# Sums for the next pair of chunks at earlier steps, a fixed order of products in every group, and a later flag matmul

## The chip, the cores and the metric

The kernel runs on one core of a Trainium2 chip. The metric is the device time of one execution in microseconds (us); for the kernel before it is 1270.25 us, the median of 3 runs (1269.96 to 1272.42). TensorE (PE) multiplies, VectorE (DVE), ScalarE (ACT) and GpSimd (POOL) do the elementwise work, and SyncE (SP) issues almost all DMAs. Each engine has one queue of instructions that it works off in order, and semaphores hold an instruction until what it needs is done.

## The reference

Three layers follow each other, all in float32:

```python
state = alpha[t] * state + k[t] v[t]^T ; y[t] = q[t] @ state        # linear attention, 4 x 8 heads, 768 x 48
x = y as [3072, 384]
h = x @ w_in ; g = where(h > 0, h, exp(min(h, 0)) - 1) ; x = g @ w_out        # w_in [384, 2048]
p = domain_probs / (domain_probs.sum(-1) + 1e-9)
for e in range(4):
    out += p[:, e:e+1] * (maximum(x @ w1[e], 0) @ w2[e])        # w1 [4, 384, 1024], w2 [4, 1024, 384]
```

## The kernel before, in words

The sequence is cut into 6 chunks of 128 positions times 4 batches, so 512 tokens are one chunk. Stage 1 (0 to about 530 us) runs attention and the first feed-forward layer. Stage 2, to which the change belongs, runs the four experts. It takes the chunks in three pairs, r = 0, 1, 2. The hidden units of all experts are cut into 32 blocks of 128, and 11 groups q = 0 to 10 take three blocks each (the last takes two). So there are 33 groups, numbered i = 11 r + q; group 12, for instance, is r = 1, q = 1.

The first product of a group (`layer1`, its matmuls are on line L810) is not done block by block, but by a scheme with fewer multiplications: 15 steps (`STEPS`; 11 steps, `STEPS2`, for q = 10), each of which multiplies one combination of weights by one combination of x and adds the product b to running tiles S0 to S5 (called `u`) or writes one of six results `c`. Results are named (m, f): half m of the tokens, block f. They come in the order (1,2) at step 5, (1,0) at step 8, (1,1) at step 10, (0,2) at step 12, (0,1) at step 13, (0,0) at step 14. All operations that read b run on VectorE, and so does S5 - at step 7 `S5 = S4 - S2`, which reads no b. Only `S1 = S1 - S4` at step 7 and `c(1,0) = S3 + S0` at step 8 run on GpSimd. At step 13 VectorE does `S1 = S1 + b`, so it needs GpSimd's S1.

The products are kept exact by splitting: every product is a main one (L810 or L870 with f32 operands, from the `xh` or `gh` tiles) and two corrections (f16 operands, from `xc` or `gc`). For a result c, ScalarE writes the main part `gh` (L755), the rectified c in place (L756) and one half of `gc` (L758), and GpSimd writes the other half of `gc` (L760).

The second product of group i - 1 (`layer2`, L870) runs interleaved with the steps of group i, as 18 items (12 for q = 10), each one main product and two corrections; the first step has no item, the second as a rule two, which read (1,0) and (1,1). `extra(n, 0)` issues items ahead of step n's matmuls and `extra(n, 1)` behind them. The switch `self.wide` decides which: when it is 0, mains go ahead, then the step's main and corrections, then the items' corrections; when it is 1, corrections go first and mains last. It flips with every step, so products of one kind lie next to each other. It is set to 0 once, at i = 0. As all groups have 15 or 11 steps, even groups begin with 0 and odd groups with 1, and the last pass (i = 33, only `layer2`) with 1.

When the last block of an expert is done, `gate` multiplies each of six banks by the probabilities on VectorE (L887) and adds it to `acc` on GpSimd (L890); for the last expert the sum is stored (L892, `out_dram`). For r = 0 that happens in groups 11 and 12.

The 15 combinations of x for the next pair are made by `prep_x(r + 1)`. It is a list of 16 pieces: piece 0 loads the raw chunk pair (`load`, L595, four DMAs into `xraw`), pieces 1 to 15 each make one combination (`one`): GpSimd adds 0 to 3 terms (L674, `xv`), two flushes later ScalarE casts it (L679, L680, `xh`), one flush after that GpSimd subtracts (L683) and SP stores it (L684, `xcd`). Groups q = 1 to 8 put in two pieces each, at steps 2 and 9. In q = 1 these are the load and combination 14, which has three additions. Only r = 0 (group 1) and r = 1 (group 12) prepare a next pair.

The order of PE, ACT, DVE and POOL is the order in which the program emits the work. SP's order is chosen by the planner of the framework, which may bring a DMA forward; once chosen, SP works it off in order too. Weights are loaded per group, `wa` (L727) and `wb` (L737) from step 0.

At the end, `flag` reduces range checks with small VectorE operations (L907 to L919), `total` sums them over the partitions by a tiny matmul (L923) into the value `ok`, which all engines read (L1306) before the program ends.

Of the kernel before, what the change touches and what calls it, by code (L numbers as in the profile page):

```python
# [95 lines left out]
class _Fast:  # L96
# [833 lines left out]
    def run(self):  # L930
# [129 lines left out]
        def second(it, ks=range(KD)):  # L1060
            g = gs[it]
            c, f = it
            self.g2a(self.w1[f // 2], f % 2, g, 512, f == 0, f == F1 - 1, ks)
            if KD - 1 in ks:
                del gs[it]
                if f == F1 - 1:
                    self.later(lambda: end1(c))
# [40 lines left out]
        for i in range(ng + 1):  # L1108
            r, q = divmod(i, NG)
            work, first_work = [], {}  # L1110
            if i:
                self.hb = ("h0", "h1")
            if i == 0:
                pieces = [(it, k) for it in items[-LA:] for k in range(KD)]
                first_work = dict(zip((4, 7, 9, 11, 13, 14), pieces))
            elif i > 0:
                work = self.layer2(i - 1, G.pop(i - 1))
            if i == ng:
                while self.queue:
                    self.flush()  # L1120
                total = self.flag()
                for n in range(0, len(work), 2):
                    if n == 4:
                        total()
                    for k in range(2):
                        for f in work[n:n + 2]:
                            f(k ^ self.wide)
                    self.flush()
                    self.wide ^= 1
                break  # L1130
            if i == 0:
                self.wide = 0
                self.hacc = self.wp.tile([128, 256], F32, tag="wt", name="hacc")
                self.hc, self.wc = 0, [0, 0]
            steps = len(STEPS if q < NG - 1 else STEPS2)
            plan = {}
            put = lambda n, f, *a: plan.setdefault(n, []).append((f, a))
            if i <= NG:
                for n, f in enumerate(self.bound_w(i)):
                    put(2 * n + 1, f)  # L1140
            if i >= 2:
                put(0, self.load_wb, i)
            if 1 <= i < ng - 1:
                put(0, self.load_wa, i + 1)
            if q in (1, 3, 6, 8):
                put(steps - 1, self.load_pb, r, (1, 3, 6, 8).index(q))
            if r + 1 < NPR:
                if q == 1:
                    xs = self.prep_x(r + 1)
                if 1 <= q <= 8:  # L1150
                    for n, s in enumerate(xs[(q - 1) * 2:q * 2]):
                        put(2 + 7 * n, do, s)
                if q == NG - 2:
                    put(4, self.load_xc, r + 1, 0)
                if q == NG - 1:
                    for j in range(1, 5):
                        put((2, 5, 8, 9)[j - 1], self.load_xc, r + 1, j)

            dve = [sum(1 for o in ops if "b" in o[2:] or o[1] == "S5") for _, ops in (STEPS if q < NG - 1 else STEPS2)]
            cum = [0]  # L1160
            for n in range(steps):
                cum.append(cum[-1] + 1 + dve[n] + (dve[n - 1] if n else 0))
            cut = [len(work) * c // cum[-1] for c in cum]

            def extra(n, k):
                for f in work[cut[n]:cut[n + 1]]:
                    f(k ^ self.wide)
                if k == 0:
                    return
                self.wide ^= 1  # L1170
                if n in first_work:
                    second(first_work[n][0], (first_work[n][1],))
                for f, a in plan.pop(n, []):
                    f(*a)

            G[i] = self.layer1(i, extra)
            assert not plan
# [186 lines left out]
```

## Time and profile before

| what | value |
|---|---|
| median of 3 runs | 1270.25 us |
| the profiled execution's own time | 1268.04 us |
| its span, first to last instruction | 1266.3 us |
| PE busy | 1226.3 us (97%), 6453 instructions |
| DVE busy | 901.2 us (71%) |
| ACT busy | 785.7 us (62%) |
| POOL busy | 555.3 us (44%) |
| mean granted TensorE clock | 0.993 of full speed |

The profile is of one execution on the chip. "Busy" is the time in which an engine worked on an instruction. PE's matmuls are pipelined, so a share of 97% says that it was rarely idle, not that it ran at its peak. The granted clock is 1.0 when TensorE has its full 2.4 GHz and 0.5 at 1.2 GHz. In rows of the timeline, the first column is the start in us from the span's start, the second the time from the first instruction's start to the last one's end, then engine, line, operation, tiles (out<-in) with shapes, and the count of instructions merged; brackets give the idle time of the engine before it and who ended it.

### The profile page before, as it was taken

What the parts mean: (1) busy time and instruction counts of PE and PEld (TensorE: products, weight loads), DVE (VectorE), ACT (ScalarE), POOL (GpSimd) and SP (SyncE); (2) the same over time, 40 slices, a digit from 0 to 9 for tenths busy, and PEclk for the clock granted to TensorE, in tenths of its full rate; (3) what the DMA queues carried; (4) which work ended last, traced back from release to release, by engine and by line L of the source; (5) the groups of instructions that cost most, each with busy time, mean ns of one, the idle gap of its engine ahead of it and who ended that gap; (6) DMA issues with size and microseconds to landing.
All of it is one profiled execution on the core that took longest, in us unless ns stands there. A gap on an engine that the chain in (4) does not pass through costs nothing. (4 is left out here: it accounts for less than half of the span.)

```text
span 1266.3 us, 18550 instructions
## 1 busy us (share of the span) xinstructions
PE 1226.3 (97%) x6453; PEld 801.3 (63%) x6457; DVE 901.2 (71%) x1478; ACT 785.7 (62%) x1624; POOL 555.3 (44%) x496
## 2 busy tenths in 40 slices
PE   8899999999999999999999999999999999999995
PEld 5677878888787888755555555555555555555553
DVE  8999687786787868866666657676766566667763
ACT  5675666766656667678787766466565455464552
POOL 0000011110111114267777957776878474456654
PEclk9899999999999999999999999999999999999998
DMA  6655356555656456735564677855555875343321
GB/s 234 234 169 170 99 194 198 191 188 188 227 199 219 159 185 218 277 125 217 180 222 162 219 253 286 291 198 219 196 203 204 301 256 191 117 177 140 143 94 53
DMA packets 78101, 246.84 MB, mean 195 GB/s; under 512 B 6840, under 2 KB 38424, under 8 KB 69936
## 3 DMA queue, kind: packets, MB, share of 16 engines
q1 hardware_dynamic: 77136, 240.87, 54.2%
q10 hardware_dynamic: 864, 4.72, 0.9%
q8 instruction: 52, 0.85, 0.3%
q14 instruction: 49, 0.40, 0.1%
HBM read 182.21 MB, written 63.36 MB: 194 GB/s over the span
## 5 line engine op out<-in xcount | busy, mean ns | idle before, releaser
L833 DVE TENSOR_TENSOR u<-h,u 128x512 f32<-128x512 f32 x258 | 177.4, 688 | 83.1 <-PE h L810 79.8
L760 POOL TENSOR_TENSOR gc_W<-c,gh_W 128x512 f16<-128x512 f32 x128 | 164.6, 1287 | 162.1 <-ACT c L756 117.6
L396 POOL TENSOR_SCALAR wh<-wc 128x384 f16<-128x384 f32 (+1 forms) x55 | 31.2, 567 | 406.6 <-ACT wh L395 349.5
L870 PEld LDWEIGHTS <-wb 128*128 128x128 f16 x1152 | 112.4, 98 | 141.3 <-issue 7.2
L755 ACT ACTIVATE gh_W<-c 128x512 fp32r<-128x512 f32 x128 | 80.3, 627 | 159.3 <-POOL c L833 85.8
L810 PE MATMUL h<-xc_Q,wa 128*128 128x512 f16 x520 | 155.6, 382 | 1.1 <-DVE c L833 0.7
L810 PE MATMUL h<-xh_Q,wa 128*128 128x512 f32 x260 | 127.0, 489 | 1.5 <-DVE u L833 1.3
L756 ACT ACTIVATE c<-c 128x512 f32<-128x512 f32 x192 | 121.1, 631 | 7.6 <-ACT gh_W L755 0.4
L810 PEld LDWEIGHTS <-wa 128*128 128x128 f16 x780 | 60.5, 98 | 100.9 <-issue 55.4
L833 DVE TENSOR_TENSOR c<-u,h 128x512 f32<-128x512 f32 x123 | 84.3, 686 | 51.2 <-PE h L810 35.2
L760 POOL TENSOR_TENSOR gc_X<-c,gh_X 128x512 f16<-128x512 f32 x64 | 82.7, 1292 | 70.9 <-ACT c L756 68.2
L462 DVE SCALAR_TENSOR_TENSOR h<-e,h 128x512 f32<-128x512 f32 x96 | 66.4, 692 | 63.9 <-ACT e L461 63.6
L827 DVE COPY u<-h 128x512 f32<-128x512 f32 x99 | 67.9, 690 | 51.5 <-PE h L810 48.4
L870 PE MATMUL t<-gc_W,wb 128*128 128x512 f16 x384 | 97.3, 379 | 0.9 <-POOL gc_W L760 0.9
L755 ACT ACTIVATE gh_X<-c 128x512 fp32r<-128x512 f32 x64 | 40.2, 627 | 80.7 <-POOL c L833 44.9
L467 ACT CAST g<-h 128x512 fp32r<-128x512 f32 x96 | 56.0, 583 | 51.1 <-DVE h L462 50.8
L468 DVE TENSOR_TENSOR g<-h,g 128x512 fp32r<-128x512 f32 x96 | 65.7, 684 | 26.0 <-ACT g L467 25.8
L460 ACT ACTIVATE e<-h 128x512 f32<-128x512 f32 x96 | 57.0, 593 | 41.1 <-PE h L451 41.0
L758 ACT CAST gc_W<-c 128x512 f16<-128x512 f32 x128 | 79.2, 619 | 4.0
L476 PE MATMUL t<-g,w_W 128*128 128x512 f32 x324 | 79.4, 389 | 0.0
L810 PE MATMUL h<-xc_W,wa 128*128 128x512 f16 x260 | 77.8, 382 | 1.1 <-DVE u L833 1.0
L890 POOL TENSOR_TENSOR acc<-acc,c 128x512 f32<-128x512 f32 x53 | 69.4, 1321 | 2.7 <-DVE c L887 2.7
(264 smaller groups left out, 2935.7 us busy)
## 6 DMA issues: line engine op xcount, KB each, us to landing
wa<-wad SPq DMA_DIRECT2D x33, 1536.0 KB, 6.7
wb<-wbd SPq DMA_DIRECT2D x30, 1536.0 KB, 7.1
raw<-in_att_dram SPq DMA_DIRECT2D x22, 964.0 KB, 5.7
wad<-wh SPq DMA_DIRECT2D x44, 384.0 KB, 2.8
wbd<-wh SPq DMA_DIRECT2D x43, 384.0 KB, 4.0
xcd<-xh SPq DMA_DIRECT2D x30, 512.0 KB, 2.9
wraw<-in_wm_dram SPq DMA_DIRECT2D x16, 768.0 KB, 5.0
wraw<-in_we_dram SPq DMA_DIRECT2D x20, 576.0 KB, 5.1
```

The costliest lines, as they stand in the source:

```text
L462: return lambda: nc.vector.scalar_tensor_tensor(out=h, in0=e, scalar=-1.0, in1=h, op0=ALU.add, op1=ALU.max)
L468: return g, lambda: nc.vector.tensor_tensor(out=g[:, 1], in0=h, in1=g[:, 0].bitcast(F32), op=ALU.subtract)
L476: nc.tensor.matmul(self.xa[k][:, 0:n], w[wl][:, fi, DM + k * 128:DM + (k + 1) * 128], g[:, gl, 0:n], start=(first and i == 0), stop=(last ...
L755: nc.scalar.activation(out=hi, in_=v, func=AF.Relu, scale=s)
L756: nc.scalar.activation(out=v, in_=v, func=AF.Relu, scale=s, accum_out=self.hacc[:, self.hc:self.hc + 1])
L758: nc.scalar.copy(cor[:, 0], v)
L760: lambda: nc.gpsimd.tensor_tensor(out=cor[:, 1], in0=v, in1=hi.bitcast(F32), op=ALU.subtract)
L810: nc.tensor.matmul(b, u, v, start=(j == 0), stop=(j == 2))
L827: nc.vector.tensor_copy(out, b)
L833: (nc.vector if "b" in (a0, a1) or dst == "S5" else nc.gpsimd).tensor_tensor(out=out, in0=val(a0, b), in1=val(a1, b), op=ALU.add if op == ...
L870: nc.tensor.matmul(oa[m, d], w, g, start=n == 0 and k == 0, stop=n == F2 - 1 and k == 2)
L890: eng.tensor_tensor(out=acc, in0=acc, in1=t, op=ALU.add)
```

## The change

Three edits, all in stage 2. (1) The pieces of `prep_x` move from steps 2 and 9 of a group to steps 1 and 4. (2) `self.wide` is set to 0 at the start of every group and of the last pass, so every group begins with main products. (3) In the last pass, `total` is emitted ahead of the last two of the 12 items instead of ahead of items 4 and 5.

```diff
@@ the last pass, i == ng @@
                 total = self.flag()
+                self.wide = 0
                 for n in range(0, len(work), 2):
-                    if n == 4:
+                    if n == 10:
                         total()
@@ the start of a group @@
             if i == 0:
-                self.wide = 0
                 self.hacc = self.wp.tile([128, 256], F32, tag="wt", name="hacc")
                 self.hc, self.wc = 0, [0, 0]
+            self.wide = 0
@@ the plan of a group @@
                 if 1 <= q <= 8:
                     for n, s in enumerate(xs[(q - 1) * 2:q * 2]):
-                        put(2 + 7 * n, do, s)
+                        put(1 + 3 * n, do, s)
```

## Rows read from the trace of the kernel before

**Rows 1.** Windows: stage 2; busy of PE, PEld, DVE, ACT, POOL, then granted clock
```profile
531.00:1226.00 695.00, 685.76 (x3068) 374.95 (x3068) 458.76 (x692) 429.32 (x921) 470.41 (x362) 1.00 0.56 200
```

**Rows 2.** Waits of PE from 545 us on: total, times, longest
```profile
PE h L810 <- DVE u L833: 3.5, 4, 1.4
PE a L870 <- POOL gc_W L760: 2.8, 3, 1.6
PE h L923 <- DVE flag_r L919: 2.2, 1, 2.2
...
PE t L870 <- POOL gc_W L760: 0.9, 1, 0.9
...
PE h L810 <- DVE u L827: 0.7, 2, 0.3
```

**Rows 3.** Timeline of SP: around group 1's raw loads, and in group 12
```profile
525.56 1.69 SPq L595 DMA_DIRECT2D xraw<-x1d  x2
...
789.67 4.08 SPq L892 DMA_DIRECT2D out_dram<-acc  x2
793.86 0.41 SPq L737 DMA_DIRECT2D wb<-wbd  x1
794.32 5.73 SPq L595 DMA_DIRECT2D xraw<-x1d  x4
```

**Rows 4.** Timeline of POOL in group 12
```profile
792.08 1.27 POOL L890 TENSOR_TENSOR acc<-acc,c 128x512 f32<-128x512 f32 x1
796.56 1.30 POOL L760 TENSOR_TENSOR gc_W<-c,gh_W 128x512 f16<-128x512 f32 x1 [3.20 <-ACT c L756]
797.81 1.77 POOL L833 TENSOR_TENSOR u<-u 128x512 f32<-128x512 f32 x1
...
804.79 1.28 POOL L674 TENSOR_TENSOR xv<-xraw 128x512 f32<-128x512 f32 x1 [1.17 <-DMA xraw<-x1d]
806.91 2.64 POOL L674 TENSOR_TENSOR xv<-xv,xraw 128x512 f32<-128x512 f32 x2 [0.84 <-DMA xraw<-x1d]
```

**Rows 5.** Timeline of DVE and of ACT at the end of group 12
```profile
806.38 0.68 DVE L833 TENSOR_TENSOR u<-h,u 128x512 f32<-128x512 f32 x1
...
800.86 0.63 ACT L755 ACTIVATE gh_W<-c 128x512 fp32r<-128x512 f32 x1 [3.73 <-POOL c L833]
...
802.80 0.62 ACT L755 ACTIVATE gh_W<-c 128x512 fp32r<-128x512 f32 x1
```

**Rows 6.** Timeline of PE at the start of groups 12 and 13
```profile
785.37 0.50 PE L810 MATMUL h<-xh_W,wa 128*128 128x512 f32 x1 [1.36 <-DVE u L833]
...
807.74 0.59 PE L810 MATMUL h<-xc_W,wa 128*128 128x512 f16 x2
...
810.84 1.02 PE L870 MATMUL a<-gc_W,wb 128*128 128x512 f16 x4 [0.70 <-POOL gc_W L760]
```

**Rows 7.** Timeline of PE and windows: two runs of nine matmuls in stage 1
```profile
81.42 2.34 PE L451 MATMUL h<-x,w_W 128*128 128x512 f32 x9
...
88.27 3.83 PE L451 MATMUL h<-x,w_W 128*128 128x512 f32 x9 [2.47 <-DVE g L468]
...
88.00:92.00 4.00, 3.73 (x10) 2.90 (x11) 3.01 (x5) 3.94 (x9) 0.00 (x0) 0.59 0.23 94
```

**Rows 8.** Timeline of POOL and PE at the end of group 1
```profile
565.76 2.63 POOL L674 TENSOR_TENSOR xv<-xv,xraw 128x512 f32<-128x512 f32 x2
...
569.66 0.59 PE L870 MATMUL a<-gc_W,wb 128*128 128x512 f16 x2 [1.56 <-POOL gc_W L760]
```

**Rows 9.** Timeline of DVE and PE in group 30
```profile
1192.74 1.68 DVE L833 TENSOR_TENSOR u<-u 128x512 f32<-128x512 f32 x1
...
1195.68 0.50 PE L810 MATMUL h<-xh_Q,wa 128*128 128x512 f32 x1 [0.56 <-DVE u L833]
```

**Rows 10.** Timeline of PE and of POOL at the end
```profile
1250.75 0.19 PE L923 MATMUL h<-flag_r 128*1 128x4 f32 x2 [2.15 <-DVE flag_r L919]
...
1251.41 6.20 POOL L890 TENSOR_TENSOR acc<-acc,c 128x512 f32<-128x512 f32 x5 [1.76 <-DVE c L887]
```

## The prediction

> **What bounds the kernel now.** I read the shares of the engines first, then the windows, then PE's waits, and last the queues of POOL and SP around the places that the edits touch. From 531 to 1226 us PE is busy for 685.76 of 695.00 us at a granted clock of 1.00, its upper level of 2.4 GHz [rows 1]: stage 2 is bound by TensorE, and a reordering can win only what PE still waits. That is little. From 545 us on the waits sum to about 12 us; POOL's `gc` accounts for 2.8 + 0.9 us, the flag for 2.2 us in one piece, and VectorE's `u` for 3.5 and 0.7 us [rows 2]. So the edits can win some 5 us at most, while one new hole on PE's path costs its full length.
>
> **Edit 1, sums at steps 1 and 4.** What it removes: at the end of group 1 the last two of three additions run for 2.63 us, `gc` comes behind them and PE waits 1.56 us [rows 8]. At step 4 these additions lie before the results begin, and the wait goes. The 0.9 us on `t<-gc_W` (group 6, after a sum at step 9) and the two waits of 0.3 us on L827 behind a full POOL should go too. I take 1.6 + 0.9 + 0.6 = 3.1 us; the bounds are 0 and 4.4 (all of POOL's 2.8 + 0.9 and L827's 0.7) [rows 2].
>
> What it moves is not only the additions. In groups 1 and 12 the first piece is the load of the raw pair and the second needs it: seven steps lay between them, now three. Stage 2's group of 15 steps takes 807.74 - 785.37 = 22.4 us [rows 6], 1.49 us a step, so the distance shrinks from 10.4 to 4.5 us. In group 1 this is harmless: its loads were issued by 527 us, long before [rows 3]. In group 12 they were not. SP issues the four loads at 794.32 to 800.05, directly behind two stores (789.67 to 793.75), which wait for GpSimd's last `acc` (792.08, done 793.35), and a `wb` load [rows 3, 4]. These stores and `wb` are emitted at step 0, before the load whether it stands at step 2 or at step 1, so I expect the loads where they were. The data came at 804.8 and 806.9, where POOL waited 1.17 and 0.84 us for it [rows 4], already late for step 9.
>
> After the change POOL reaches the additions when `acc` is done, at 793.35, waits until 804.8, and is through at 806.91 + 2.64 = 809.55. Queued behind, at 1.3 us each [rows 4]: `gc(1,2)` until 810.8 (before, it ran at 796.56), the `xh` difference until 812.1, S1 until 813.4 (before, from 797.81), `c(1,0)` until 814.7. VectorE needs S1 at step 13, which it did at 806.38 [rows 5]; now it does so at 813.4, done 814.1. PE needs the bank that this frees for the first step of group 13: 814.1 instead of 807.74 [rows 6], 6.4 us. ScalarE is behind `c(1,0)` too: its results follow at 802.80 - 800.86 = 1.94 us [rows 5], so c(1,0) is rectified at 816.0 and (1,1) at 817.9, and GpSimd's `gc(1,1)` is done at 819.2. Group 13 with mains first has its first corrections right behind the first step, so PE waits for that as well, then has two corrections (0.45), the step's three products (0.67) and two mains (0.45) to do, at 685.76 / 3068 = 0.224 us a matmul [rows 1]: 820.8. Before, this point was reached at 810.84 + 0.45 = 811.3 [rows 6]. The price is 9.5 us, group 13's own wait of 0.70 included. Bounds: -0.7 (the data are early, as in group 1) and 9.5; I take 9.5, since the loads' row in group 12 is the nearest.
>
> **TensorE's clock after that hole.** In stage 1, nine matmuls took 2.34 us, and nine like them 3.83 us after PE had waited 2.47 us; the granted clock of that stretch was 0.59, so for most of it the lower level, 1.2 GHz [rows 7]. A hole of 6.4 us, followed by two shorter ones, should do the same: 3.83 - 2.34 = 1.5 us more; bounds 0 (waits of up to 1.6 us in stage 2 left the clock at 1.00 [rows 1, 2]) and 3.0 (twice). The Trainium skill (TensorE: Matmul & The Clock Gate, Why this matters for your kernels) advises against gaps between bursts of matmuls because the clock falls, which speaks against this edit; by it alone the 1.5 us would be owed for the 6.4 us hole and not for the short ones. The rows agree on both.
>
> The moved pieces' other instructions: ScalarE's casts and SP's stores come five steps earlier, where ScalarE idles (3.73 us before a result [rows 5]); at nothing, as PE waits for no weight load that stands behind such a store [rows 2]. But the `xh` difference now lies at step 7, beside VectorE's S5, which reads two SBUF tiles. Group 30 shows such a meeting: S5 took 1.68 us, where such an operation takes 0.68 [rows 5], while POOL ran, a gate followed, and PE waited 0.56 us at step 10 [rows 9].
>
> **Edit 2, mains first.** Odd groups now run like even ones. In these, products of steps 7 and 8 come close together, which is where PE waited for `u` in gate groups (0.56 in group 30). Corrections of the second step are also needed 1.1 us earlier (0.67 + 0.45). I count three more waits of 0.6 us, for gate groups that become even-like or get the `xh` difference beside S5: 1.8 us. Bounds: -0.5 (odd groups' own waits go) and 4.8 (all eight such gate groups: 3, 11, 17, 19, 25 and 8, 14, 6). The order changes kind once more per border, 32 times; kinds change at every step already without a visible wait, so 0.2 us, bounds 0 and 1.
>
> **Edit 3, the flag.** PE no longer stands 2.15 us for the flag's sum [rows 10]. But GpSimd's five additions run back to back from 1251.41 to 1257.61, and they begin when the first gate is done, behind the flag's operations on VectorE, which stay. So the stores become bound by POOL, about half a microsecond before VectorE's last addition now ends (1257.23 + 0.93). With the mains ahead of `gc` I take 0.8 us; bounds -2.2 and +0.3 (`ok` is written some 2 us later, still before the last store).
>
> **Sum.** 9.5 + 1.5 - 3.1 + 1.8 + 0.2 - 0.8 = +9.1 us. The profiled execution took 1268.04 us (span 1266.3 and 1.7 around it), so 1277.1 by its measure. It lies 2.2 us under the median of the runs shown; on that median the sum gives 1279.4 us, which is my forecast.
>
> **Rivals.** (A) *The loads are early.* If SP takes the four loads ahead of the two stores, nothing of the hole is left. The place is SP's queue in group 12. The point: POOL must be through with `gc(1,1)` by 809.5 or so (it follows the additions by 9.7 us), so with the additions by 799.8, 9.75 us earlier than 809.55; so the loads have to begin by about 784.6 instead of 794.32. For it: SP brought group 1's loads forward by more than a group. Against: it did not do so in group 12, with the same freedom. Time: -0.7 - 3.1 + 1.8 + 0.2 - 0.8 = -2.6, 1267.7 us, faster. (B) *The loads come between the two stores*, behind the first (790.1), as the second waits for `acc`: 4 us earlier, so 9.5 becomes 5.5, and the sum 5.1: 1275.4 us. (C) *The small terms cancel*: the loads early, few of POOL's waits gone and more of S5's meetings: 1270 us. (D) *S5's meetings dominate* on top of the hole: 4.8 for 1.8, 1282.4 us.
>
> **How the numbers follow.** Forecast 0.56 (own range 1275.5 to 1282), D 0.05, B 0.12, A 0.19, C 0.08. The range of 1269 to 1283 leaves out most of A and little above, about 2 in 10. A measurement of this kernel can tell about 0.2%, 2.5 us, from no change: slower takes the forecast, D and B without its low end, 0.72; faster takes 0.12 of A, whose 2.6 us lies at the bound; the same takes the rest of A, C and B's low end, 0.16.
>
> **What would show it.** Right: in group 12 POOL stands some 11 us for `xraw` ahead of its first `xv`; PE stands 6 us at the start of group 13 and again at its first corrections, and the granted clock falls there; the wait at 569.66 is gone; L923 no longer waits 2 us. Wrong: SP issues group 12's loads before 785, or POOL's S1 is done before 806; or waits of 0.6 us at step 10 show in many groups.

## The result and the profile after

The changed kernel takes 1287.34 us (median of 4 runs, 1285.58 to 1288.78), the kernel before 1270.11 us beside it (4 runs). The ratio is 1.0135, interval 1.0112 to 1.0157. It became slower, as forecast, but by nearly twice the forecast +9.1 us, and above the range. A second set of 4 runs (e8 below) gave 1283.24 us and a ratio of 1.0115 (1.0081 to 1.0149). Two executions below, 4145 us in e7 (the one that was profiled) and 1771 us in e9, were in a slow state: the medians hold them, the ratios do not.

The profiled execution took 1288.01 us, 19.97 more than the one before. Cutting both traces at the first product of a group (three L810 matmuls a step) shows where:

| part | before | after | difference | forecast |
|---|---|---|---|---|
| stage 1 (start of group 0) | 529.03 | 533.88 | +4.85 | none |
| groups 12 and 13 | 45.21 | 55.27 | +10.06 | +11.0 (hole 9.5, clock 1.5) |
| groups 6 to 9 | 89.98 | 94.44 | +4.46 | |
| groups 16 to 20 | 111.48 | 113.68 | +2.20 | |
| group 2 | 23.73 | 22.41 | -1.32 | |
| groups 0 to 31 less these | 426.34 | 425.73 | -0.61 | |
| the four rows above together | | | +4.73 | -1.1 |
| from the start of group 32 to the end of the span | 40.53 | 40.79 | +0.26 | -0.8 |
| around the span | 1.74 | 1.81 | +0.07 | |

First the view that bounds, stage 2 (busy of PE, PEld, DVE, ACT, POOL, granted clock, DMA share, GB/s), answering to [rows 1]: PE is idle for 18.4 of 715 us (before 9.2 of 695), and the clock is 0.99.

```profile
531.00:1246.00 715.00, 696.57 (x3090) 378.14 (x3089) 462.71 (x695) 432.49 (x929) 469.39 (x363) 0.99 0.55 197
```

PE's waits from 550 us on (total, times, longest), answering to [rows 2]:

```profile
PE h L810 <- DVE u L833: 10.0, 9, 4.3
PE a L870 <- POOL gc_W L760: 4.3, 5, 1.6
PE t L870 <- POOL gc_W L760: 1.7, 3, 1.2
PE a L870 <- POOL gc_X L760: 1.1, 2, 0.8
PE h L810 <- DVE c L833: 0.7, 1, 0.7
PE h L810 <- DVE u L827: 0.5, 1, 0.5
```

One wait of 4.3 us is new, which is the hole. The flag's line has gone. But GpSimd's `gc`, of which I forecast that 2.5 us would go, now costs 7.1 us in 10 waits, against 4.8 in 6: to the 3.7 in 4 of [rows 2] come two lines of before on `gc_X`:

```profile
PE a L870 <- POOL gc_X L760: 0.8, 1, 0.8
...
PE t L870 <- POOL gc_X L760: 0.3, 1, 0.3
```

The hole, in SP's queue in group 12 (answers to [rows 3]):

```profile
795.68 6.58 SPq L892 DMA_DIRECT2D out_dram<-acc  x3
802.37 0.41 SPq L737 DMA_DIRECT2D wb<-wbd  x1
802.82 3.70 SPq L595 DMA_DIRECT2D xraw<-x1d  x4
```

Group 12 begins at 793.87 us here and at 785.37 before [rows 6]. The loads begin 8.95 us into it in both: they stayed behind the stores, as forecast. GpSimd in the same group (answers to [rows 4]):

```profile
800.59 1.27 POOL L890 TENSOR_TENSOR acc<-acc,c 128x512 f32<-128x512 f32 x1
811.48 1.28 POOL L674 TENSOR_TENSOR xv<-xraw 128x512 f32<-128x512 f32 x1 [9.61 <-DMA xraw<-x1d]
813.61 2.64 POOL L674 TENSOR_TENSOR xv<-xv,xraw 128x512 f32<-128x512 f32 x2 [0.86 <-DMA xraw<-x1d]
...
817.43 1.26 POOL L683 TENSOR_TENSOR xh<-xv,xh 128x512 f16<-128x512 f32 x1
818.65 1.26 POOL L833 TENSOR_TENSOR u<-u 128x512 f32<-128x512 f32 x1
```

It stands 9.61 us for the raw data, and S1 (`u<-u`) is behind it. PE at the start of group 13 (answers to [rows 6]), and the windows after its long wait (columns as in the stage 2 row above):

```profile
820.69 0.80 PE L810 MATMUL h<-xh_W,wa 128*128 128x512 f32 x1 [4.28 <-DVE u L833]
...
823.96 1.01 PE L870 MATMUL a<-gc_W,wb 128*128 128x512 f16 x2 [1.59 <-POOL gc_W L760]
825.89 1.01 PE L870 MATMUL a<-gc_W,wb 128*128 128x512 f16 x2 [0.92 <-POOL gc_W L760]
```

```profile
821.00:826.00 5.00, 2.49 (x6) 0.69 (x6) 1.15 (x2) 4.67 (x10) 2.68 (x3) 0.50 0.86 314
826.00:831.00 5.00, 5.00 (x14) 2.48 (x13) 1.53 (x3) 4.79 (x11) 3.19 (x3) 0.55 0.00 0
```

PE stops three times, and its clock is at the lower level to about 830.5 us.

The tail (answers to [rows 10]): L923, the flag's matmul, no longer waits in its row, but GpSimd's five additions begin where they did, 25.66 us after the start of group 32 (before 25.64), and take 6.62 instead of 6.20 us.

```profile
1272.12 0.19 PE L923 MATMUL h<-flag_r 128*1 128x4 f32 x2
...
1271.07 6.62 POOL L890 TENSOR_TENSOR acc<-acc,c 128x512 f32<-128x512 f32 x5 [1.76 <-DVE c L887]
```

### The profile page after: what moved, and what is told of

It is laid out like the page before. It is cut to its first block, busy times and chain, and to the rows that moved or that the text cites. A ratio compares the mean times of both kernels' runs of the same rounds, so it can differ in the third digit from the quotient of the medians.

```text
span 1286.2 us, 18582 instructions
## 1 busy us (share of the span) xinstructions
PE 1236.4 (96%) x6453; PEld 805.1 (63%) x6457; DVE 902.7 (70%) x1478; ACT 785.5 (61%) x1624; POOL 554.2 (43%) x496
## 4 chain that ended last, share of the span: by engine, by line
PE 62%; POOL 13%; DVE 9%; ACT 8%; issue 5%; DMA 2%; SPq 0%; POOLq 0%; DVEq 0%; ACTq 0%
PE h L810 15%; PE t L476 12%; PE h L451 12%; PE t L870 8%; PE a L870 7%; PE h L870 3%; POOL acc L890 3%; POOL gc_W L760 3%; ACT c L756 2%; POOL xh L683 2%; POOL c L833 2%; ACT gh_W L755 1%; POOL xv L674 1%; PE a L259 1%; POOL u L833 1%
## 5 line engine op out<-in xcount | busy, mean ns | idle before, releaser
L810 PE MATMUL h<-xc_Q,wa 128*128 128x512 f16 x520 | 155.6, 382 | 0.0
L810 PE MATMUL h<-xh_Q,wa 128*128 128x512 f32 x260 | 129.1, 497 | 3.8 <-DVE u L833 2.4
L810 PEld LDWEIGHTS <-wa 128*128 128x128 f16 x780 | 60.7, 98 | 97.3 <-issue 50.9
L827 DVE COPY u<-h 128x512 f32<-128x512 f32 x99 | 68.0, 690 | 71.4 <-PE h L810 69.7
L810 PE MATMUL h<-xc_W,wa 128*128 128x512 f16 x260 | 79.2, 387 | 0.0
L810 PE MATMUL h<-xh_W,wa 128*128 128x512 f32 x130 | 68.0, 523 | 7.8 <-DVE u L833 7.8
```

The lines of the kernel that those rows point to most:

```text
L810: nc.tensor.matmul(b, u, v, start=(j == 0), stop=(j == 2))
L827: nc.vector.tensor_copy(out, b)
```

## The experiments

My theory after the result: the late loads make the hole, and the 4.73 us elsewhere come from both edits together (sums that delay GpSimd's S1, and corrections that odd groups need earlier). The rivals were that one of the two edits makes them alone. "Stage 2" below is the time from the start of group 0 to that of group 32 in each kernel's profiled execution, 696.74 us for the kernel before and 711.53 for the changed one (711.31 in e8, the same kernel, so 0.2 us is the scatter that was seen).

| kernel | median us (before beside it) | ratio, interval | stage 2 | groups 6-9 | 12+13 | 16-20 |
|---|---|---|---|---|---|---|
| e1, only edit 1 | 1285.85 (1270.44) | 1.0120, 1.0097 to 1.0142 | 711.99 | 93.81 | 55.80 | 113.63 |
| e2, only edit 2 | 1271.64 (1270.44) | 1.0012, 0.9998 to 1.0026 | 697.23 | 90.99 | 44.43 | 112.35 |
| e3, only edit 3 | 1270.59 (1270.44) | 1.0007, 0.9993 to 1.0022 | 696.77 | 90.04 | 45.22 | 111.49 |
| e4, after + early loads | 1274.56 (1270.44) | 1.0026, 1.0009 to 1.0043 | 700.56 | 94.38 | 44.53 | 113.67 |
| e5, e4 with steps 1, 2 | 1270.82 (1269.77) | 1.0005, 0.9990 to 1.0020 | 697.95 | 92.82 | 44.19 | 113.29 |
| e6, e4 with steps 1, 9 | 1271.62 (1269.77) | 1.0023, 1.0003 to 1.0042 | 697.57 | 91.78 | 44.17 | 112.43 |
| e7, e4 + late differences | 1268.82 (1269.77) | 0.9984, 0.9969 to 0.9999 | - | - | - | - |
| e8, after again | 1283.24 (1269.77) | 1.0115, 1.0081 to 1.0149 | 711.31 | 94.41 | 55.22 | 113.63 |
| e9, e7 again | 1269.35 (1269.95) | 0.9978, 0.9964 to 0.9993 | 693.49 | 90.07 | 44.19 | 111.55 |
| e10, e9 without edits 2, 3 | 1267.00 (1269.95) | 0.9972, 0.9960 to 0.9984 | 692.83 | 89.62 | 44.39 | 110.77 |
| e11, after + late differences | 1276.08 (1269.95) | 1.0059, 1.0040 to 1.0078 | 703.43 | 90.06 | 53.68 | 111.96 |

**One edit at a time.** Each takes its hunk of the diff and leaves the others as before.

> Only edit 1 (sums at steps 1 and 4; order of kinds and flag as before). Theory: the hole of groups 12/13 comes from this edit alone, 9 to 10 us; and the other 4.7 us (waits at the borders after groups 6 to 8 and 16 to 19) need both edits, so about half of them, those at borders into even groups, stay: +11 to +12 us over the kernel before, with PE waiting for gc at the starts of groups 8, 18 or 20. Rival: the small waits come from mains-first alone: then only the hole less the wait of group 2 that goes, +8 to +9 us. Rival: the small waits come from this edit alone: +14 us. Stage 1 should start its last part (group 0) anywhere from 528 to 535 us, as the clock falls there, whatever the edit; if the kernel's edits set it, 529.

Measured: +15.4 us on the median, +15.25 in stage 2. Groups 12 and 13 have +10.59 of it, groups 6 to 9 and 16 to 20 +5.98. So my theory that the small waits need both edits fell: this edit alone makes them, the third case of the expectation.

> Only edit 2 (every group and the last pass begin with mains; sums at steps 2 and 9). No hole in groups 12/13 (PE's longest wait there under 1.5 us). Theory that the small waits need both edits: +1 us (0 to +2). Rival, they come from mains-first alone: +4.7 us, with the waits at the starts of groups 7 and 9 seen here too. Forecast of the prediction for this part: +2.0 us (1.8 + 0.2).

Measured: +0.49 us in stage 2, +1.2 on the median with a ratio whose interval holds 1. Mains-first alone is nearly harmless, also for the start of group 13.

> Only edit 3 (the flag's matmul ahead of the last two items). PE's 2.2 us wait on L923 goes. Theory from the tail after the change (40.79 us against 40.53 from the start of the last pass's items to the end): GpSimd's additions and the last store set the end, so 0.0 us (-0.3 to +0.3). Forecast of the prediction: -0.8 us. Rival, the wait counts in full: -2.2 us.

Measured: nothing, stage 2 +0.03 and the tail 40.71 us against 40.53. PE's 2.2 us for the flag did not set the end in the kernel before. In e1 and e2, which lack edit 3, it did in part: the granted clock fell behind this wait, and the tails took 41.60 and 41.84 us (e1's rows are in the last section). The eight profiled kernels with edit 3 take 40.70 to 40.93, and e10, again without it, 40.87 at a clock of 1.00. So the edit removes a wait that, in two of the four profiled executions without it, was followed by a lower clock and about 1 us more of tail.

**The loads.** e4 is the changed kernel with

```diff
-                if q == 1:
+                if q == 1 - r:
                     xs = self.prep_x(r + 1)
+                    if r:
+                        put(0, do, xs[0])
+                        xs[0] = []
```

> All three edits, but the raw loads for the third pair are emitted at step 0 of group 11 instead of step 1 of group 12; nothing else changes. Theory (late loads make the hole): the four loads begin before 785 us, GpSimd's first sum of group 12 waits for nothing, PE's wait at the start of group 13 falls from 4.3 us to under 1, the clock doesn't fall there, and the kernel is 9 to 11 us faster than the changed one: +6 to +8 us over the kernel before. Rival (GpSimd's sums themselves, ahead of S1, make the hole, with the loads only adding): at least 4 us of waits stay in groups 12/13, +11 us or more. Rival (the load collides with other transfers and the weights come late): waits for wa or wb appear on PE in groups 11 to 13.

SP and GpSimd of e4 around group 12:

```profile
774.98 10.96 SPq L595 DMA_DIRECT2D xraw<-x1d  x4
786.04 13.94 SPq L892 DMA_DIRECT2D out_dram<-acc  x6
...
799.53 1.29 POOL L674 TENSOR_TENSOR xv<-xraw 128x512 f32<-128x512 f32 x1
```

SP takes the loads ahead of all six stores, GpSimd's first sum waits for nothing, and groups 12 and 13 shrink by 55.27 - 44.53 = 10.74 us. At the start of group 13, at 813.76 us, PE has no wait and its full clock:

```profile
814.00:819.00 5.00, 5.00 (x24) 2.71 (x23) 2.76 (x5) 4.61 (x11) 3.37 (x3) 1.00 1.03 425
```

The hole is the late loads. What is left, +3.82 us in stage 2, is the small waits. It is less than the +6 to +8 that I expected, since I had taken 9 to 11 us off a median of +17.2, of which stage 2 and the tail account for 15.05 (see stage 1 below).

**What the small waits are.** First the second piece's step:

```diff
-                        put(1 + 3 * n, do, s)
+                        put(1 + n, do, s)        # e5; in e6: put(1 + 8 * n, do, s)
```

> The changed kernel with the early loads, and the second piece of each group at step 2 instead of step 4 (put(1 + n)). Its difference then lies about two steps ahead of GpSimd's S1 instead of directly ahead. Theory (the second piece, directly ahead of S1 and c(1,0), makes the waits at the borders after groups 6 to 9 and 16 to 20): most of the 4 us go, gate groups 8 and 19 keep some, as GpSimd is full there: stage 2 at +1 us over the kernel before (0 to +2). Rival (the first piece, at step 1 beside the gc of the group before, makes them): unchanged or worse, +4 us or more. Rival (mains-first makes them): unchanged, +4 us.

> The changed kernel with the early loads, and the second piece back at step 9 (put(1 + 8 * n)): only the first piece moves, from step 2 to 1. Theory (the second piece's place ahead of S1 makes the 4 us): stage 2 as with mains-first alone, +0.5 us (0 to +1.5), with the wait at the start of group 2 back. Rival (the first piece): +3 us or more.

Measured in stage 2: e5 +1.21, e6 +0.83 us, so the second piece at step 4 is what costs. But in e5, where I expected most of the waits to go, those at the starts of groups 7, 18 and 20 stayed or grew (1.55, 1.05 and 0.94 us; in the changed kernel 1.28, 0.80 and 0.94): it is not enough that the difference lies further ahead of S1. Here is the end of group 6 on GpSimd, before:

```profile
671.84 1.27 POOL L833 TENSOR_TENSOR u<-u 128x512 f32<-128x512 f32 x1
673.07 1.28 POOL L833 TENSOR_TENSOR c<-u 128x512 f32<-128x512 f32 x1
675.84 1.27 POOL L760 TENSOR_TENSOR gc_W<-c,gh_W 128x512 f16<-128x512 f32 x1 [1.50 <-ACT c L756]
677.08 1.30 POOL L674 TENSOR_TENSOR xv<-xraw 128x512 f32<-128x512 f32 x1
678.34 1.28 POOL L760 TENSOR_TENSOR gc_W<-c,gh_W 128x512 f16<-128x512 f32 x1
679.56 1.29 POOL L683 TENSOR_TENSOR xh<-xv,xh 128x512 f16<-128x512 f32 x1
```

and after, with what PE waited at the start of group 7:

```profile
676.14 1.27 POOL L890 TENSOR_TENSOR acc<-acc,c 128x512 f32<-128x512 f32 x1
677.37 1.28 POOL L683 TENSOR_TENSOR xh<-xv,xh 128x512 f16<-128x512 f32 x1
678.61 1.28 POOL L833 TENSOR_TENSOR u<-u 128x512 f32<-128x512 f32 x1
679.85 1.28 POOL L833 TENSOR_TENSOR c<-u 128x512 f32<-128x512 f32 x1
682.62 1.28 POOL L760 TENSOR_TENSOR gc_W<-c,gh_W 128x512 f16<-128x512 f32 x1 [1.50 <-ACT c L756]
685.06 1.27 POOL L760 TENSOR_TENSOR gc_W<-c,gh_W 128x512 f16<-128x512 f32 x1 [1.16 <-ACT c L756]
...
686.38 0.59 PE L870 MATMUL a<-gc_W,wb 128*128 128x512 f16 x2 [1.28 <-POOL gc_W L760]
```

Before, the sum and the difference lay behind `c(1,0)` (`c<-u`), beside waits for ScalarE. After, the sum lies further up and the difference directly ahead of S1. This is a gate group, in which GpSimd works without a break up to `c(1,0)`. My reading at this point was that every instruction put ahead of S1 delays `c(1,0)` by its 1.25 us, ScalarE's and GpSimd's chain of results follows (1.94 us for each), and PE waits for `gc(1,1)`. Behind `c(1,0)` GpSimd idles 1.50 us, then 1.16. So I put the difference there (a flush stands at the start of every step, so two flushes are two steps):

```diff
-            self.later(low, 3)
+            self.later(low, 5)
```

> The changed kernel with the early loads, and every difference xh two flushes later, so the second one comes behind c(1,0), where GpSimd idles about 1.5 us, while its sum stays at step 4. Splits the second piece: if the difference alone is what delays S1, stage 2 is at +0.5 us over the kernel before; if the sum alone, at +3.8 as without this edit; I expect both, as GpSimd works there without a break in gate groups and each takes 1.25 us: +2 us (1 to 3).

The runs came out 1 us under the kernel before, where I expected 2 over it. The kernel ran again for its profile (e9), beside e10, which has the sums of edit 1, the early loads and the late differences, but edits 2 and 3 not, and e11, the changed kernel with the late differences alone.

> The changed kernel with the early loads and every difference xh two flushes later, once more, for its profile. In the run before it came out 1 us under the kernel before where I expected 2 us over it. New theory: the difference directly ahead of S1 and c(1,0) is the whole cause of the small waits, the sum at step 4 is none; then stage 2 is 695 to 696 us (before 696.7), GpSimd's c(1,0) is followed by the difference in the 1.5 us in which it waited for ScalarE, and the waits of PE at the starts of groups 7, 8 and 18 are gone; 1 to 2 us faster than before. Rival: stage 2 is at 698 us or more and the median of that run was luck of stage 1.

> As the one before without mains-first and without the flag's edit: sums at steps 1 and 4, early loads, differences two flushes later. If mains-first costs 0.5 us here as it did alone: 0.5 us less than the one before, so 1.5 to 2.5 us under the kernel before, stage 2 at 694.5 to 695.5 us. Rival: mains-first gains once the differences are out of the way: stage 2 0.5 us longer than the one before.

> The changed kernel with only the differences two flushes later, the raw loads where the change has them. Theory (two separate causes that add): the small waits go, the hole of groups 12 and 13 stays but for the 1.25 us of one difference that no longer lies ahead of S1: +8 to +9.5 us over the kernel before, 55.2 us less 1 to 2 for groups 12 and 13 together (44.5 with early loads). Rival (the difference is what makes the hole long): groups 12 and 13 under 50 us, +4 us or less.

The same place in e9:

```profile
676.13 1.28 POOL L833 TENSOR_TENSOR u<-u 128x512 f32<-128x512 f32 x1
677.37 1.27 POOL L833 TENSOR_TENSOR c<-u 128x512 f32<-128x512 f32 x1
678.60 1.28 POOL L683 TENSOR_TENSOR xh<-xv,xh 128x512 f16<-128x512 f32 x1
680.14 1.30 POOL L760 TENSOR_TENSOR gc_W<-c,gh_W 128x512 f16<-128x512 f32 x1 [0.26 <-ACT c L756]
682.58 1.27 POOL L760 TENSOR_TENSOR gc_W<-c,gh_W 128x512 f16<-128x512 f32 x1 [1.15 <-ACT c L756]
```

The difference now fills the gap, and ahead of the `gc` behind it GpSimd waits only 0.26 us more. Stage 2 is 7.07 us shorter than e4's, by nothing but the later differences: more than the 3.82 that had to be explained, since waits that the kernel before has go too (group 2 takes 22.01 us, before 23.73). The sums are still ahead of S1, so they alone do not make the waits. The edit moves the first pieces' differences too, from step 4 to step 6; e6, with these at step 4 and the second piece back at step 9, was only 0.83 us above before. It also takes the difference away from VectorE's S5, but that is not what gained: PE's waits behind S5 at step 10 grew, from 0.48 us (group 8 of e4) to 0.68 and 0.69 (groups 8 and 19 of e9). The waits at the starts of groups 8 and 18 are gone, that of group 7 is down to 0.32 us; with this the theory held. In stage 2 the gain over before was more than the 1 to 2 us expected (3.25). e10 is 0.66 us shorter still in stage 2: mains-first costs about that much, as it did alone (0.49). e10 is the fastest of all, 1267.00 against 1269.95 us, though the interval of its ratio overlaps that of e9. Its waits on PE from 550 us on:

```profile
PE h L810 <- DVE u L833: 4.0, 5, 1.4
PE h L923 <- DVE flag_r L919: 2.2, 1, 2.2
PE a L870 <- POOL gc_X L760: 0.8, 1, 0.8
PE a L870 <- POOL gc_W L760: 0.5, 1, 0.5
PE t L870 <- POOL gc_W L760: 0.3, 1, 0.3
PE t L870 <- POOL gc_X L760: 0.3, 1, 0.3
```

`gc` is down to 1.9 us, from 4.8 in the kernel before. e11 has both causes apart: its small waits are e9's, its groups 12 and 13 take 53.68 us, with this wait on GpSimd:

```profile
801.65 1.27 POOL L674 TENSOR_TENSOR xv<-xraw 128x512 f32<-128x512 f32 x1 [9.60 <-DMA xraw<-x1d]
```

Stage 2 is 6.69 us over before; e9's -3.25 and the hole's 53.68 - 44.19 = 9.49 add to 6.24. I expected 8 to 9.5 on the median and it was +6.1, because I expected less of the late differences.

**Whether the edits change stage 1.**

> The changed kernel once more, beside the others. Its stage 2 should again be 14.8 us longer than before (14 to 15.5) and its tail 0.3 us, as stage 2 hardly varies; where stage 1 ends varies from 528 to 536 us from execution to execution with the clock. So on the median +15 us over the kernel before, 1285.5, not the +17.2 of the first four runs. Rival (the edits make stage 1 longer): +17 us or more.

Measured: stage 2 +14.57 us, as expected, and group 0 at 529.23. The median, expected at +15, came out at +13.5 us; this and the +17.2 of the first four lie on both sides of stage 2's and the tail's 14.9 to 15.1. In the profiled executions group 0 begins at 528.62 (e3), 528.84 (e11), 529.03 (before), 529.23 (e8), 531.71 (e4), 533.25 to 534.17 (e6, e10, after, e9, e5), 534.61 (e1) and 535.43 (e2): the same changed kernel stands at either end. So the +4.85 us of stage 1 are not the change's.

## Why the prediction was wrong

The sum was +9.1 us; stage 2 and the tail became 15.05 us longer. Of the 5.95 between them the small terms are 5.83 and the flag 1.06, less 0.94 for the hole and the clock. The remaining 2.2 us of the first median's +17.2 are not the change's: they belong to the scatter of stage 1.

**The hole: right, within 1 us, in part by luck.** The loads came where I put them, and GpSimd, VectorE, PE and ScalarE were late in the order that I gave. Group 12 begins 8.50 us later than before; with this shift I forecast S1 done at 821.9 us and it was at 819.91, and PE's first matmul at 822.6, which came at 820.69, because the four loads were issued in 3.70 us instead of 5.73 and the wait was 9.61 us instead of 11.45. The clock cost more in turn: from 825.89 to 830.55 us PE did 11 matmuls in 4.66 us, which at the forecast's 0.224 us are 2.46: 2.2 us for 1.5. Together 10.06 us against 11.0. Of this the hole itself is what is left, some 7.9 us for 9.5; the two errors cancel in part.

**The small terms: wrong in sign, and the step that failed.** It is the step that put the moved pieces' casts and stores "at nothing" and then priced the `xh` difference at step 7 only as a neighbour of VectorE's S5. I had followed GpSimd's queue for group 12, difference included, and did not do so for the fifteen other groups with pieces. There the second piece's difference stands directly ahead of S1 and `c(1,0)`, and in and around gate groups that queue has no slack. The term is missing from the sum. What I gave as -1.1 us became +4.73, and e9 beside e4 shows what the place is worth: 7.07 us, for nothing but the differences two flushes later.

**The removed waits (3.1 us).** Group 2 became 1.32 us shorter, of 1.6: the wait that stood at 569.66 [rows 8] is down to 0.23 us. Of the others nothing went: `t<-gc_W`, 0.9 us before, is 1.7 in 3 waits, and L827 0.5 for 0.7. With the differences out of the way most of it goes (1.9 us of `gc` in e10, 4.8 before, and no L827). I had counted on a removal while adding as much ahead of the same instructions.

**S5's meetings and the order of kinds (1.8 + 0.2 us).** Mains-first costs 0.49 alone and 0.66 with the late differences, less than the 2.0. At step 10 the change has one new wait, 0.50 us in group 8, where S5 took 1.62 us against 0.93 before. Rival D (these meetings dominate) gave 1282.4 us, near the second set's 1283.24, by a mechanism that was not the one.

**The flag (-0.8 us).** Nothing (+0.26). I had written that the stores would become bound by GpSimd just before VectorE's end; the additions' start did not move at all. That the wait for the flag can lower the clock, as in e1 and e2, I had not considered.

**Rival A** (early loads, no hole) was tried as e4: the loads ahead of 784.6 us remove the hole, as said, but its time would have been 4 us above the kernel before instead of 2.6 below, for the same missing term.

**Stage 1** has no term in the sum and needs none; but medians of four runs lie up to 2.2 us off, and in the profiled executions stage 1 is where such differences lie.

## What to carry to other kernels

When a piece is moved on an engine that works in order, write down what stands behind each of its instructions at the new place in every group, not only where a transfer makes it late: an engine that is 44% busy over the span had no slack where it counted. A piece that nobody waits for soon belongs behind the instruction that others wait for, into a gap that this engine has anyway; here a delay of two flushes was worth 7 us. And a load belongs ahead of the stores that wait for results, before its first reader is moved closer.

## What the runs showed of the hardware

Stage 1 differs by up to 6.8 us between executions with the same order of instructions on PE there. Of the 12 profiled ones, the four with a granted clock of 1.00 from 14 to 22 us end it at 528.62 to 529.23 us, the eight with 0.53 to 0.79 at 531.71 to 535.43. Windows of 14 to 22 us, first of the changed kernel, then of the kernel before:

```profile
14.00:22.00 8.00, 7.78 (x55) 6.11 (x56) 6.31 (x9) 4.50 (x8) 0.00 (x0) 0.57 0.46 156
```

```profile
14.00:22.00 8.00, 7.29 (x75) 6.14 (x76) 7.96 (x12) 5.85 (x12) 0.00 (x0) 1.00 0.65 224
```

PE is as busy in both, but at 0.57 it gets through 55 matmuls and at 1.00 through 75. Why the clock falls there in one execution and not in another stays open.

After the hole the clock stayed at its lower level for most of 4.7 us in which PE had work without a break (0.55 from 826 to 831), so this hole cost more than its length. The Trainium skill (TensorE: Matmul & The Clock Gate, Why this matters for your kernels) puts such a fall down to an idle gap between bursts of matmuls. The traces agree as far as they go: 4.28 us of waiting stand ahead of this fall (3.03 us in e11, where it fell as well), while a wait of 1.55 us at the start of group 7 in e5 left the clock at 1.00 (its row, then the window around it):

```profile
685.30 0.59 PE L870 MATMUL a<-gc_W,wb 128*128 128x512 f16 x2 [1.55 <-POOL gc_W L760]
```

```profile
680.00:690.00 10.00, 8.45 (x38) 4.54 (x37) 5.15 (x8) 9.61 (x22) 5.36 (x6) 1.00 0.66 263
```

Between these lengths the traces do not settle it. Behind the flag's wait of 2.15 us the clock fell in e1, and behind one of 2.63 us in e2; behind the same 2.15 us in the kernel before [rows 10] it stayed at 1.00. First e1's row and the window from it on, then the window of the kernel before:

```profile
1271.57 0.19 PE L923 MATMUL h<-flag_r 128*1 128x4 f32 x2 [2.15 <-DVE flag_r L919]
```

```profile
1271.60:1275.60 4.00, 4.00 (x13) 2.14 (x14) 2.19 (x6) 0.00 (x0) 2.78 (x3) 0.58 0.19 68
```

```profile
1250.80:1254.80 4.00, 4.00 (x20) 2.33 (x21) 2.85 (x7) 0.00 (x0) 3.39 (x3) 1.00 0.19 65
```

PE is busy throughout in both and gets through 13 matmuls at the one clock and 20 at the other.
